# One weight matrix of a decode step, loaded as 7 rows per partition plus three small loads in place of 8 rows per partition

## The chip, the cores and the metric

The kernel runs on one core of one Trainium2 chip. The time is the device time of one execution in microseconds (us). Before the change three runs took 400.60, 400.62 and 400.72 us, with a median of 400.62 us. A separate execution was recorded by the hardware profiler and took 400.47 us. All durations and points in time below come from that one execution and are counted from the start of its span.

## The reference

One token `x` of 1024 numbers goes through a layer norm, then through two branches whose results are added to it. All arrays are bf16.

```python
xn = layernorm(x)
return x + A(xn) + B(xn)

# A: attention over a cache, 32 query heads, 4 key/value heads, 65536 keys of 128 numbers
q = xn @ wq                                   # wq [1024, 4096]
p = softmax(q @ k_cache.T * 128 ** -0.5)      # k_cache, v_cache [4, 65536, 128]
A = (p @ v_cache) @ wo                        # wo [4096, 1024]

# B: a small mixer and a two-layer net
h  = gelu(layernorm(xn) @ w1)                 # w1 [1024, 1024]
g0..g3 = the four quarters of h, each shifted along the sequence by 1, -1, 2, -2, zeros moved in
hs = concatenate(g0..g3) @ w2                 # w2 [1024, 1024]
x1 = xn + hs
B  = x1 + gelu(layernorm(x1) @ w3) @ w4       # w3 [1024, 3584], w4 [3584, 1024]
```

The sequence has length 1, so every shift moves the only token out and a zero in. The left operand of the product with `w2` is therefore a vector of zeros for all inputs. The kernel still loads `w1` and `w2` and does both products, with `g_col`, a column of zeros, as the left operand of the second.

## The kernel before

The kernel reads 169.87 MB once and computes on it while it streams in. On-chip memory holds three buffers, `slot0` to `slot2`, each of 128 partitions by 32768 bf16 values (64 KB per partition, 8 MB in all). A fixed list, `stream`, says what goes through them: `wq`, `w3`, `w12` (`w1` and `w2` side by side in one slot), then for each of 8 units u a block of keys `K u` and a block of values `V u`, each filling a slot, then `wo` and `w4` (in five pieces of 8, 12, 5, 2 and 1 rows per partition). Item i of the list goes to slot i modulo 3.

The kernel writes its work down as one list of operations, `Program`, and then `plan` works out the waits. Each operation has regions that it reads and regions that it writes. The function `region` turns an access into a tensor name, an interval of partitions and an interval of bytes in a partition, and `meet` says whether two regions overlap. An operation waits for every earlier operation of another queue whose region it must not overtake: a write waits for an earlier write to an overlapping region and for earlier readers of it. Each load counts as a queue of its own, so two loads into overlapping regions are ordered by a wait of the second for the landing of the first. The waiting is done by the engine that issues.

All large loads are issued by SyncE (the queue SP), strictly in the order of the list. `load` issues the loads of one item, and `freed(it)` issues the load of the item three places further on, which goes to the same slot, and which therefore waits for the last matmul that reads the item `it`. At the start SP issues `wq`, `w3`, `w1` and `w2` with nothing to wait for. Then comes `K0`, which goes into the slot of `wq` and waits for `compute_wq`; then `V0`, which waits for `compute_w3`; then `K1`, which waits for `compute_w12`; and so on to the end. The tiny load of `x` is issued by ScalarE.

TensorE also works in the order of the list: `compute_wq` (64 matmuls), `compute_w3` (64), `compute_w12` (16 with `w1`, then 16 with `w2`), then unit by unit `scores`, `maxima`, `weights` and `values`. `row_acc` is the helper that adds a product of one column with a 512-wide piece of a weight matrix to the accumulator `psB`. `w2` uses it with all 128 partitions, and so do `wo` and the larger part of `w4` at the end. In `compute_w12` a row number m*8+c of `w2` lies on partition m, as the c-th row there, and the loop runs over c. VectorE transposes the keys in place, reduces and transposes; ScalarE does the exponentials. GpSimd (POOL) sets some constants at the start, `g_col` the last of them, and later places the queries.

All instructions that the list records have the line of a helper: L82 for the vector engines, L89 for loads, L93 for the store, L102 for weight loads of TensorE and L106 for its matmuls.

Of the kernel before, what the change touches and what calls it, by code (L numbers as in the profile page):

```python
# [7 lines left out]
BF16 = mybir.dt.bfloat16  # L8
F32 = mybir.dt.float32
# [5 lines left out]
P = 128  # L15
ROW = 32768
# [3 lines left out]
NARROW = 8  # L20
AHEAD = 5

WIDTH = {F32: 4, BF16: 2}


def region(ap):

    dims, size = list(ap.ap), WIDTH[ap.dtype]
    pitch, rows = dims[0]
    at = ap.offset % pitch  # L30
    last = at + sum((n - 1) * s for s, n in dims[1:])
    p0 = ap.offset // pitch
    return ap.tensor.name, p0, p0 + rows, at * size, (last + 1) * size


def meet(a, b):
# [3 lines left out]
class Op:  # L40
    def __init__(self, engine, emit, reads, writes, alone=False, transfer=False):
        self.engine, self.emit, self.alone, self.transfer = engine, emit, alone, transfer
        self.reads = [region(a) for a in reads]
        self.writes = [region(a) for a in writes]
        self.waits = []
        self.awaited = False


class Program:
# [45 lines left out]
    def mm(self, out, lhsT, rhs, start, stop, pos=(0, 0), size=(P, P)):  # L95

        pe, nc = self.engines["pe"], self.nc
        what = (str(lhsT), size)
        if any(s != size for (_, s), _ in self.held.values()):
            self.held.clear()  # L100
        if pos not in self.held or self.held[pos][0] != what:
            self.add(Op("pe", lambda: pe.ldweights(lhsT, tile_position=pos), [lhsT], []))  # L102
            self.held[pos] = (what, region(lhsT))

        def emit():
            return pe.add_instruction(mybir.InstMatmult(  # L106
                name=nc.get_next_instruction_name(), engine=mybir.EngineType.PE, start_tensor_calc=start,
                stop_tensor_calc=stop, tile_size=size, tile_position=pos, ldweights=False, bass_skip_group_check=True,
                ins=[pe.lower_ap(rhs), pe.lower_ap(lhsT)], outs=[pe.lower_ap(out)]))
        return self.add(Op("pe", emit, [rhs, lhsT], [out]))  # L110
# [96 lines left out]
def kernel(  # L207
# [15 lines left out]
    D = A_x.shape[-1]  # L223
# [6 lines left out]
    DC = D // P  # L230
    FC = F // P
    UKEYS = P * ROW // DH
    assert DH == P and HQ // HKV == 8 and HKV == 4 and D == 1024 and F == 3584 and S == 1
    assert SK == 2 * UKEYS and sum(W4_PIECES) == FC
    NB = 2
    NU = HKV * NB
    SCALE = float(DH) ** -0.5
    LEAD = 8 * (SETS - 1)
    COLS = (P, 32)

    prog = Program(nc)
    pe, dve, act, pool = prog, prog.dve, prog.act, prog.pool

    def sb(name, shape, dtype=F32):
        return nc.alloc_sbuf_tensor(name, list(shape), dtype)

    def ps(name, shape):
        return nc.alloc_psum_tensor(name, list(shape), F32)
# [11 lines left out]
    g_col = sb("g_col", [P, 1], BF16)  # L260
# [14 lines left out]
    sc = ps("sc", [P, SUBS, 512])  # L275
    oacc = ps("oacc", [P, 512])
    pm = [ps(f"pm{i}", [P, 512]) for i in range(2)]
    psB = ps("psB", [P, 512])
# [7 lines left out]
    tiles = {it: slots[i % 3] for i, it in enumerate(stream)}  # L286

    def load(it):
        t = tiles[it]
        if it == "wq":  # L290
            prog.load("sp", t[:], A_wq.rearrange("(p c) n -> p (c n)", c=DC))
        elif it == "w3":
            prog.load("sp", t[:, 0:DC * F], B_w3.rearrange("(p c) f -> p (c f)", c=DC))
        elif it == "w12":
            prog.load("sp", t[:, 0:DC * D], B_w1.rearrange("(p c) n -> p (c n)", c=DC))
            prog.load("sp", t[:, DC * D:2 * DC * D], B_w2.rearrange("(m c) n -> m (c n)", c=DC))
        elif it == "wo":
            prog.load("sp", t[:], A_wo.rearrange("(p j) n -> p (j n)", p=P))
        elif it == "w4":
            w4_v = B_w4.rearrange("(m c) n -> m c n", c=FC)  # L300
            c0 = 0
            for n in W4_PIECES:
                prog.load("sp", t[:, c0 * D:(c0 + n) * D], w4_v[:, c0:c0 + n, :].rearrange("p c n -> p (c n)"))
                c0 += n
        else:
            kind, i = it
            g, b = divmod(i, NB)
            cache = A_k_cache if kind == "K" else A_v_cache
            prog.load("sp", t[:], cache[0, g, b * UKEYS:(b + 1) * UKEYS, :].rearrange("(p ct) d -> p (ct d)", p=P))

    def freed(it):

        n = stream.index(it) + 3
        if n < len(stream):
            load(stream[n])

    load("wq")
    opening = len(prog.ops)

    dve.memset(x_row[:], 0.0)  # L320
    prog.load("act", x_row[0:1, :], A_x[0, 0:1, :])
    load("w3")
    load("w12")

    pool.memset(ident_f[:], 0.0)
    pool.affine_select(out=ident_f[:], in_=ident_f[:], compare_op=ALU.not_equal, fill=1.0, base=0,
# [11 lines left out]
    pool.memset(x_halves[:], 0.0)  # L338
    pool.memset(qdiag[:], 0.0)
    pool.memset(g_col[:], 0.0)  # L340

    def row_acc(j, lhsT, rhs, start=False):
        return pe.mm(psB[32 * j:32 * j + 32, :], lhsT.to_broadcast([P, 32]), rhs, start, False, (0, 32 * j), COLS)

    x_t = p_sb[:, 0:DC * 32].rearrange("p (c j) -> p c j", j=32)
    for a in range(4):
# [4 lines left out]
    def layernorm(src, tag):  # L351
        rowsum = sb(f"ln_rowsum_{tag}", [P, 1])
        dve.reduce_sum(out=rowsum[:], in_=src[:], axis=AX.X)
        at = next_pm()
        pe.mm32(at[:, 0:1], ones_f[:], rowsum[:], True, True)
        negmean = sb(f"ln_negmean_{tag}", [P, 1])
        dve.tensor_scalar(out=negmean[:], in0=at[:, 0:1], scalar1=-1.0 / D, scalar2=None, op0=ALU.mult)
        cen = sb(f"ln_cen_{tag}", [P, DC])
        dve.tensor_scalar(out=cen[:], in0=src[:], scalar1=negmean[:, 0:1], scalar2=None, op0=ALU.add)
        sq = sb(f"ln_sq_{tag}", [P, DC])  # L360
        rowsq = sb(f"ln_rowsq_{tag}", [P, 1])
        dve.tensor_tensor_reduce(out=sq[:], in0=cen[:], in1=cen[:], scale=1.0, scalar=0.0,
                                 op0=ALU.mult, op1=ALU.add, accum_out=rowsq[:])
        pe.mm32(at[:, 1:2], ones_f[:], rowsq[:], True, True)
        std = sb(f"ln_std_{tag}", [P, 1])
        act.activation(out=std[:], in_=at[:, 1:2], func=ACTF.Sqrt, bias=eps_t[:, 0:1], scale=1.0 / D)
        rstd = sb(f"ln_rstd_{tag}", [P, 1])
        dve.reciprocal(out=rstd[:], in_=std[:])
        normed = sb(f"ln_out_{tag}", [P, DC])
        dve.tensor_scalar(out=normed[:], in0=cen[:], scalar1=rstd[:, 0:1], scalar2=None, op0=ALU.mult)  # L370
        rep = sb(f"ln_rep_{tag}", [P, DC, 32], BF16)
        dve.tensor_copy(out=rep[:], in_=normed[:].unsqueeze(2).to_broadcast([P, DC, 32]))
        return normed, rep, negmean, rstd

    xn, xn_rep, negmean1, rstd1 = layernorm(xT, "a")
    _, xn2_rep, _, _ = layernorm(xn, "b")
# [51 lines left out]
        dve.tensor_copy(out=hT[:], in_=h_row[:, ::32])  # L428

    def compute_w12():  # L430
        wt = tiles["w12"][:, 0:2 * DC * D].rearrange("p (w c n) -> p w c n", w=2, c=DC)
        for c in range(DC):
            for q in range(2):
                pe.mm(sc[0:32, q, :], xn2_rep[:, c, :], wt[:, 0, c, 512 * q:512 * (q + 1)], c == 0, c == DC - 1,
                      (0, 0), COLS)
        h1 = p_sb[0:32, 0:1024].rearrange("p (q n) -> p q n", q=2)
        act.activation(out=h1, in_=sc[0:32, 0:2, :], func=ACTF.Gelu_apprx_tanh)
        for c in range(DC):
            for j in range(2):
                row_acc(j, g_col[:], wt[:, 1, c, 512 * j:512 * (j + 1)], start=(c == 0))  # L440
        freed("w12")

    W = ROW // SETS

    nball = [sb(f"nball{i}", [P, NB]) for i in range(2)]
    lall = [sb(f"lall{i}", [P, NB]) for i in range(2)]
    mx = sb("mx", [P, 1])
    m8 = sb("m8", [1, 8])
    rep = sb("rep", [1, P])
    negmg = sb("negmg", [P, 1])  # L450
    wb = sb("wb", [P, NB])
    lw = sb("lw", [P, NB])
    rl = sb("rl", [P, 1])
# [70 lines left out]
    compute_wq()  # L524
    compute_w3()
    compute_w12()
    for u in range(NU):
        g, b = divmod(u, NB)
# [15 lines left out]
    for j in range(32):  # L544
        for h in range(2):
            row_acc(h, oT[:, j:j + 1], tiles["wo"][:, D * j + 512 * h:D * j + 512 * (h + 1)])
    wt = tiles["w4"]
    for c in range(FC - NARROW):
        for j in range(2):
            row_acc(j, hT[:, c:c + 1], wt[:, D * c + 512 * j:D * c + 512 * (j + 1)])  # L550
# [66 lines left out]
```

## Time and profile before

| What | us |
|---|---|
| median of three runs | 400.62 |
| the profiled execution | 400.47 |
| its span | 399.2 |
| `wq` issued by SP, seen as landed by TensorE | 0.94, 22.78 |
| `w3`, `w1` and `w2` issued by SP | 2.31 to 3.67 |
| `K0` issued by SP, seen as landed by VectorE | 28.84, 70.17 |
| `V0` and `K1` issued by SP | 52.21 and 57.92 |
| the store issued | 397.99 |

The profiled execution lies 0.15 us under the median of the runs, and 1.27 us of it lie outside the span. The profile names engines PE (TensorE), PEld (its weight loads), DVE (VectorE), ACT (ScalarE), POOL (GpSimd) and SP (SyncE); a "q" behind a name is the engine's sequencer, which issues DMAs. In the digits by slices each of the 40 digits is the busy share of a fortieth of the span (10 us) in tenths. The names of buffers are given without their numbers, so `slot` is any of the three slots, and `in_B_w_dram` stands for `w1`, `w2`, `w3` and `w4`.

### The profile page before, as it was taken

To read this page: it belongs to the slowest core of one execution; us is meant where nothing else is said; L and a number is where in the kernel's file an instruction comes from. 1 tells how busy PE (TensorE), PEld (TensorE's weight loads), DVE (VectorE), ACT (ScalarE), POOL (GpSimd) and SP (SyncE) were. 2 spreads that over 40 slices of the span, in tenths; PEclk is the share of its full clock that TensorE was granted. 3 is DMA by queue.
4 is the path that set the end of the run, shared out by engine and by line. 5 is a ranking of instruction groups with operands and counts; after the bars stand their busy time and mean duration, and the time that the engine had idled before them with its cause. 6 is when DMAs were issued, how large, how long until landed. Compare 5 with 4: busy or idle time off the path is not lost.

```text
span 399.2 us, 2557 instructions
## 1 busy us (share of the span) xinstructions
PE 223.5 (56%) x1360; PEld 45.8 (11%) x890; DVE 210.2 (53%) x156; ACT 27.6 (7%) x35; POOL 6.2 (2%) x29
## 2 busy tenths in 40 slices
PE   0260970592469256923874196529652946393687
PEld 0210010010100020001001000201020102000233
DVE  0521010975096549653963795259439942793411
ACT  1010030002000200020002000200010011002000
POOL 2000000000000000000000000000000000000000
PEclk9995795598869666978796889568867995698669
DMA  8989999999999999999999999999999999999996
GB/s 329 506 374 419 470 420 427 421 453 479 415 420 427 420 429 427 460 460 420 415 427 420 440 427 455 453 420 420 427 429 440 427 460 435 420 420 427 402 439 259
DMA packets 3760, 170.03 MB, mean 426 GB/s; under 512 B 419, under 2 KB 421, under 8 KB 678
## 3 DMA queue, kind: packets, MB, share of 16 engines
q1 hardware_dynamic: 3744, 169.87, 98.7%
q8 instruction: 9, 0.15, 0.1%
q14 instruction: 1, 0.01, 0.0%
q10 hardware_dynamic: 6, 0.00, 0.0%
HBM read 169.87 MB, written 0.00 MB: 426 GB/s over the span
## 4 chain that ended last, share of the span: by engine, by line
DMA 56%; DVE 24%; PE 14%; another core or an unknown queue 2%; ACT 2%; issue 0%; SPq 0%
DMA slot<-in_A_k_cache_dram 42%; DVE slot L82 19%; PE sc L106 9%; DMA slot<-in_B_w_dram 9%; DMA slot<-in_A_wq_dram 5%; PE oacc L106 4%; DVE p_sb L82 2%; DVE mx L82 2%; ACT p_sb L82 2%; PE pm L122 1%; DVE m L82 0%; DVE rep L82 0%; DVE nball L82 0%; DVE x_halves L82 0%
## 5 line engine op out<-in xcount | busy, mean ns | idle before, releaser
L82 DVE STREAM_TRANSPOSE slot<-slot 128x4096 f32<-128x4096 f32 x32 | 139.4, 4411 | 52.2 <-DMA slot<-in_A_k_cache_dram 52.2
L106 PE MATMUL sc<-slot,qdiag 128*128 128x512 bf16 x512 | 128.2, 410 | 69.0 <-DVE slot L82 68.9
L106 PE MATMUL oacc<-slot,p_sb 128*32 128x512 bf16 x512 | 46.3, 542 | 37.5 <-DVE p_sb L82 18.7
L82 DVE STREAM_TRANSPOSE p_sb<-p_sb 128x2048 bf16<-128x2048 bf16 (+2 forms) x10 | 20.8, 2084 | 38.4 <-ACT p_sb L82 38.3
L82 DVE TENSOR_REDUCE mx<-sc 128x1 f32<-128x2048 f32 x8 | 18.3, 2291 | 29.7 <-PE sc L106 29.7
L102 PEld LDWEIGHTS <-qdiag 128*128 128x128 bf16 x128 | 13.0, 102 | 180.0 <-issue 180.0
L82 ACT ACTIVATE p_sb<-sc,nball 128x2048 bf16<-128x2048 f32 x8 | 15.7, 1967 | 249.9 <-DVE nball L82 249.9
L102 PEld LDWEIGHTS <-p_sb 128*32 128x32 bf16 x512 | 17.3, 131 | 63.3 <-issue 21.8
L106 PE MATMUL sc<-slot,ln_rep_b 128*32 128x512 bf16 (+1 forms) x80 | 16.2, 832 | 8.8 <-DMA slot<-in_B_w_dram 8.6
L82 DVE SCALAR_TENSOR_TENSOR og<-oacc,wb,og 128x512 f32<-128x512 f32 x4 | 3.0, 750 | 19.9 <-PE oacc L106 19.9
L122 PE MATMUL pm<-ident_f,mx 128*1 128x128 f32 x8 | 2.3, 283 | 19.1 <-DVE mx L82 19.1
L106 PE MATMUL psB<-slot,oT 128*32 128x512 bf16 x64 | 9.3, 463 | 1.3 <-DVE oT L82 1.3
L116 PE MATMUL pm<-ol,selx 128*128 128x129 f32 x8 | 2.6, 414 | 10.6 <-DVE ol L82 10.6
L106 PE MATMUL sc<-slot,ln_rep_a 128*32 128x512 bf16 x64 | 6.0, 559 | 4.2 <-DMA slot<-in_A_wq_dram 4.2
L116 PE MATMUL pm<-ln_rowsum_a,msk 128*128 128x1 f32 x2 | 0.6, 363 | 13.5 <-DVE ln_rowsum_a L82 13.5
L82 DVE TENSOR_TENSOR og<-psB,slot 64x512 f32<-64x512 f32 x1 | 0.7, 683 | 13.2 <-PE psB L106 13.2
L82 POOL COPY qdiag<-qx 32x32 bf16<-32x32 bf16 x16 | 3.2, 202 | 277.2 <-PE sc L106 250.5
L82 DVE STREAM_TRANSPOSE p_sb<-x_row 32x256 bf16<-32x256 bf16 x4 | 2.5, 616 | 7.6 <-DMA x_row<-in_A_x_dram 7.6
L122 PE MATMUL pm<-ident_f,rep 1*128 1x1 f32 x8 | 1.9, 235 | 5.0 <-DVE rep L82 5.0
L82 ACT COPY og<-oacc 128x512 f32<-128x512 f32 x4 | 2.3, 585 | 32.9 <-PE oacc L106 32.9
L82 DVE CAST p_sb<-sc 128x512 bf16<-128x512 f32 x1 | 0.7, 691 | 7.4 <-PE sc L106 7.4
L106 PE MATMUL psB<-slot,hT 128*32 128x512 bf16 x40 | 4.5, 379 | 0.0
(86 smaller groups left out, 63.1 us busy)
## 6 DMA issues: line engine op xcount, KB each, us to landing
slot<-in_B_w_dram SPq DMA_DIRECT2D x1, 7168.0 KB, 37.4
slot<-in_B_w_dram SPq DMA_DIRECT2D x3, 2048.0 KB, 43.4
slot<-in_B_w_dram SPq DMA_DIRECT2D x1, 3072.0 KB, 34.5
slot<-in_B_w_dram SPq DMA_DIRECT2D x1, 1280.0 KB, 33.5
slot<-in_B_w_dram SPq DMA_DIRECT2D x1, 512.0 KB, 34.4
slot<-in_B_w_dram SPq DMA_DIRECT2D x1, 256.0 KB, 34.5
slot<-in_A_k_cache_dram SPq DMA_DIRECT2D x8, 42.1
slot<-in_A_v_cache_dram SPq DMA_DIRECT2D x8, 36.9
```

The source lines that it names most:

```text
L82: return program.add(Op(engine, lambda: method(*args, **kw), reads, writes, alone=kw.get("accum_out") is not None))
L102: self.add(Op("pe", lambda: pe.ldweights(lhsT, tile_position=pos), [lhsT], []))
L106: return pe.add_instruction(mybir.InstMatmult(name=nc.get_next_instruction_name(), engine=mybir.EngineType.PE, start_tensor_calc=start, st ...
L116: return self.add(Op("pe", lambda: pe.matmul(out, lhsT=lhsT, rhs=rhs, start=start, stop=stop, tile_position=pos, skip_group_check=True), [ ...
L122: return self.add(Op("pe", lambda: pe.transpose(out, in_, identity), [in_, identity], [out]))
```

## The change

`w1` stays as it is. Of `w2`, rows 0 to 895 are laid out with 7 rows on each of the 128 partitions. The other 128 rows go to the columns behind, in three loads: 16 partitions (0, 4, 8 to 60) with 3 rows each, 5 partitions (2, 6 to 18) with 7 rows each, and 3 partitions (1, 5, 9) with 15 rows each. The columns behind are set to zero first, over partitions 0 to 63 and 15 rows, by one memset on GpSimd; the three loads write over a part of that. The item's loads are written down after the constants of GpSimd now. The product with `w2` takes 7 steps over all partitions and 15 steps over the first 64 partitions, in place of 8 steps, each step being two matmuls. `region` now understands accesses that step over partitions, and gives them the interval from the first to the last partition touched.

```diff
+W2_ROWS = 7
+W2_EXTRA = ((0, 4, 16, 3), (2, 4, 5, 7), (1, 4, 3, 15))
+
 def region(ap):
     dims, size = list(ap.ap), WIDTH[ap.dtype]
-    pitch, rows = dims[0]
+    stride, rows = dims[0]
+    pitch = stride
+    if ap.tensor.name.startswith("slot"):
+        pitch = ROW * WIDTH[BF16] // size
     at = ap.offset % pitch
     last = at + sum((n - 1) * s for s, n in dims[1:])
     p0 = ap.offset // pitch
-    return ap.tensor.name, p0, p0 + rows, at * size, (last + 1) * size
+    return ap.tensor.name, p0, p0 + (rows - 1) * (stride // pitch) + 1, at * size, (last + 1) * size
...
+    W2_REST = (DC + W2_ROWS) * D
...
         elif it == "w12":
             prog.load("sp", t[:, 0:DC * D], B_w1.rearrange("(p c) n -> p (c n)", c=DC))
-            prog.load("sp", t[:, DC * D:2 * DC * D], B_w2.rearrange("(m c) n -> m (c n)", c=DC))
+            prog.load("sp", t[:, DC * D:W2_REST], B_w2[0:P * W2_ROWS, :].rearrange("(m c) n -> m (c n)", c=W2_ROWS))
+            k0 = P * W2_ROWS
+            for p0, step, k, c in W2_EXTRA:
+                prog.load("sp", t[p0:p0 + step * k:step, W2_REST:W2_REST + c * D],
+                          B_w2[k0:k0 + k * c, :].rearrange("(m c) n -> m (c n)", c=c))
+                k0 += k * c
+            assert k0 == D
...
     load("w3")
-    load("w12")
...
     pool.memset(g_col[:], 0.0)
-
-    def row_acc(j, lhsT, rhs, start=False):
-        return pe.mm(psB[32 * j:32 * j + 32, :], lhsT.to_broadcast([P, 32]), rhs, start, False, (0, 32 * j), COLS)
+    more = max(c for _, _, _, c in W2_EXTRA)
+    pool.memset(tiles["w12"][0:64, W2_REST:W2_REST + more * D].bitcast(F32), 0.0)
+    load("w12")
+
+    def row_acc(j, lhsT, rhs, start=False, k=P):
+        return pe.mm(psB[32 * j:32 * j + 32, :], lhsT.to_broadcast([k, 32]), rhs, start, False, (0, 32 * j), (k, 32))
...
     def compute_w12():
-        wt = tiles["w12"][:, 0:2 * DC * D].rearrange("p (w c n) -> p w c n", w=2, c=DC)
+        wt = tiles["w12"]
         for c in range(DC):
             for q in range(2):
-                pe.mm(sc[0:32, q, :], xn2_rep[:, c, :], wt[:, 0, c, 512 * q:512 * (q + 1)], c == 0, c == DC - 1,
+                pe.mm(sc[0:32, q, :], xn2_rep[:, c, :], wt[:, D * c + 512 * q:D * c + 512 * (q + 1)], c == 0, c == DC - 1,
                       (0, 0), COLS)
...
-        for c in range(DC):
+        for c in range(W2_ROWS):
             for j in range(2):
-                row_acc(j, g_col[:], wt[:, 1, c, 512 * j:512 * (j + 1)], start=(c == 0))
+                row_acc(j, g_col[:], wt[:, D * (DC + c) + 512 * j:D * (DC + c) + 512 * (j + 1)], start=(c == 0))
+        for c in range(more):
+            for j in range(2):
+                row_acc(j, g_col[0:64, :], wt[0:64, W2_REST + D * c + 512 * j:W2_REST + D * c + 512 * (j + 1)], k=64)
         freed("w12")
```

## The prediction

> **What bounds the kernel now.** I read the page's busy shares first, then the digits by slices and the DMA queues, then the start of the chain of waits, then the order in which SP issues, and last the single DMA packets in the trace.
>
> ```profile
> PE 223.5 (56%) x1360; PEld 45.8 (11%) x890; DVE 210.2 (53%) x156; ACT 27.6 (7%) x35; POOL 6.2 (2%) x29
> ...
> DMA  8989999999999999999999999999999999999996
> ...
> q1 hardware_dynamic: 3744, 169.87, 98.7%
> q8 instruction: 9, 0.15, 0.1%
> q14 instruction: 1, 0.01, 0.0%
> q10 hardware_dynamic: 6, 0.00, 0.0%
> ```
>
> No compute engine is busy for more than 56% of the span, while SP's queue (q1) keeps the 16 DMA engines busy for 98.7% of it. The kernel is a stream of loads; an idle microsecond of all DMA engines is a microsecond of the result unless a later stage has slack. The next view is the chain of waits up to 75 us, then SP's queue in order of time:
>
> ```profile
> 0.94 21.80 DMA slot<-in_A_wq_dram
> 22.74 0.04 issue
> 22.78 6.04 PE sc L106 x50
> 28.82 0.02 issue
> 28.84 41.31 DMA slot<-in_A_k_cache_dram
> 70.15 0.02 issue
> 70.17 8.77 DVE slot L82 x2
> ```
> ```profile
> 2.31 1.36 SPq L89 DMA_DIRECT2D slot<-in_B_w_dram  x3
> 28.84 0.33 SPq L89 DMA_DIRECT2D slot<-in_A_k_cache_dram  x1
> 52.21 0.33 SPq L89 DMA_DIRECT2D slot<-in_A_v_cache_dram  x1
> 57.92 0.33 SPq L89 DMA_DIRECT2D slot<-in_A_k_cache_dram  x1
> 91.31 0.33 SPq L89 DMA_DIRECT2D slot<-in_A_v_cache_dram  x1
> ```
>
> The reader is to see that K0 is issued at 28.84 and lands 41.31 us later, although its own 8 MB need about 19.4 us (8 packets of 64 KB per engine at 2.42 us). For the other 20 us it stands in the queue behind w3, w1 and w2. That early issue keeps the engines from ever running dry there. The trace's packet records, chained to 16 engines (a packet belongs to the engine whose last packet ends where it begins), give, from the earliest to the latest engine:
>
> ```text
> load      first packet     last data
> w1        38.95 - 39.32    43.81 - 44.18
> w2        43.82 - 45.01    48.68 - 50.36
> K0        48.68 - 50.36    68.00 - 69.72
> last w4   394.15 - 396.05  394.81 - 396.69
> ```
>
> Each load begins where the one before ends, on every engine. The only pauses are the instruction fetches of q8 (16 KB, about 1.05 us each); each sets one engine back by about 1.5 us (a gap of 1.0, and 0.5 on the packet after it). Eight of them fall on eight different engines; the first, at 44.0, makes the slow end of w2. The undelayed engines end at 394.81, the fetching ones at about 396.4 to 396.7, and the kernel ends with the latest.
>
> **The change part by part.**
>
> *Fewer bytes of w2 on every engine.* An engine carried 8 packets of 16 KB (611 ns each). It now carries 8 of 14 KB (about 537 ns, between the 389 ns of the 10 KB packets and the 611) and one of 6 KB (about 236 ns, from 161 ns for 4 KB and 389 for 10). 8 x 611 - 8 x 537 - 236 = 0.35 us less before the next load. That is the whole possible gain, 0.09% of the time, and only if engines without a fetch take the rest. What tells no change from a gain in this kernel is about 0.2%, or 0.8 us.
>
> *The three small loads wait for each other.* They touch different partitions, but `region` gives each one an interval: partitions 0 to 60, 2 to 18 and 1 to 9, all beginning at the same column. The intervals overlap, each load is a queue of its own, so `plan` makes the load of 5 partitions wait for the landing of the load of 16, and the load of 3 for that of 5. SP issues in order, and queued behind on SP are K0, V0 and all that follows. K0 can no longer be issued at 28.84; it comes after two landings, and the first is behind w2 in the same queue. The DMA engines run dry. Step by step, taking the nearest row for each:
>
> - The load of 16 ends on the slowest engine at 50.36 - 0.35 = 50.01.
> - From last data to the waiter: wq 22.40 to 22.78 and the last w4 piece 396.69 to 397.16, so 0.38 to 0.47; I take 0.42.
> - From SP's issue to the first packet of an idle queue: 1.01 for wq on the earliest engine (0.94 to 1.95), 1.34 on the latest; the store took 0.74 (397.99 to 398.73). I take 1.01, a load from SP being the nearer row.
> - The load of 5: 14 KB per engine, 0.54 us at full rate. A packet after a fetch gap takes 0.5 longer, wq's first ones 0.56 to 0.94 longer. Bounds 0.54 and 1.48; I take 1.04, the fetch gap being as short as this pause.
> - Landing to SP: 0.42 again. The load of 3 is issued; SP takes 0.33 to 0.50 per issue (three in 1.36 at 2.31); 0.40. Then K0 is issued and its first packet comes 1.01 later.
>
> K0's earliest packet: 50.01 + 0.42 + 1.01 + 1.04 + 0.42 + 0.40 + 1.01 = 54.31, against 48.68. K0 begins cold: wq's first packets take 3180 ns in place of 2420, so 0.76 more (bounds 0 and 0.94). Sum: 54.31 - 48.68 + 0.76 = 6.4 us. By the lower ends (0.38, 0.74, 0.54, 0.38, 0.33, 0.74, 0) it is 4.4, by the upper ones (0.47, 1.34, 1.48, 0.47, 0.50, 1.34, 0.94) it is 7.9.
>
> Why no more is lost or regained by the fetch delays: before, the first fetch's delay stayed on its engine. Now the load of 16 must land on all engines, so all wait for that engine (this is in the sum, which starts at 50.01), and they start K0 together. The later fetches set other engines back again, so the end still lies about 1.9 us behind an undelayed engine, as before (396.69 against 394.81).
>
> [...]
>
> *The load of 3.* 30 KB go ahead of K0 on three engines (1.13 us), but its packets start an issue (0.40) earlier, so these engines enter K0 0.73 us behind the others. If they get no later fetch, this hides under the 1.5 us that a fetch costs elsewhere: 0. If one does, it adds 0.73. The engine that carried the one-row load of x shows a gap of 76 ns at 7.8 us and no fetch; I take 0.
>
> *The memset, and the wait of the load of 16 for it.*
>
> ```profile
> L82 POOL MEMSET qdiag<- 128x536 bf16 x1 | 0.5, 544 | 0.1
> L82 POOL MEMSET ident_f<- 128x128 f32 x1 | 0.2, 204 | 1.9 <-POOLq L577 1.9
> L82 POOL MEMSET g_col<- 128x1 bf16 x1 | 0.1, 102 | 0.1
> ```
>
> About 0.8 ns an element ((544 - 102) / 536), so 7680 fp32 elements take 6.2 us, from 5.6 to about 11.9. POOL is next needed at 31.54. The load of 16 stands behind w3, w1 and w2, whose data run to 48.7, so its wait until 11.9 is covered. If the memset held up VectorE's preparation (10.56 to about 16.5), 6 us of cover remain before wq lands at 22.78. Price 0.
>
> *More matmuls with w2.* 16 become 44.
>
> ```profile
> L106 PE MATMUL psB<-slot,g_col 128*32 128x512 bf16 x16 | 2.7, 380 | 0.0
> ```
>
> 2.7 / 16 = 0.17 us each, overlapped; 28 more are 4.8 us, and without overlap (380 ns) 10.6. K1 waits for them: issued at 57.92 before, now at 62.7, at most about 69. Its data cannot move before V0's have, which was 87.33 on the earliest engine and is later now. Price 0, with 18 us of cover at the least; TensorE has nothing else until K0 lands. V0, free since 52.21, is issued right behind K0.
>
> Nothing downstream gives the 6.4 us back: every later load is queued well before its predecessor ends (V1 at 91.31, its first packet at 106.68), so the stream has no gap to close, and it shifts whole. Against the profiled execution: 400.47 + 6.4 = 406.9; from the median, 0.15 above that execution, 407.0.
>
> **The rivals.**
>
> *The small loads fall on one engine each.* The store's two rows made two overlapping packets, the load of x one; loads of 5 and 3 rows are not in the trace. On one engine, 70 KB take 2.6 us in place of 0.54 (+2.1), and 90 KB hold K0 back there by 3.4 - 0.4 = 3.0, of which 1.5 may hide under fetches. 400.6 + 6.4 + 2.1 + 1.5 = 410.6. For it: no row of such a shape. Against: the store spread its rows.
>
> *An engine with the load of 3 also gets a fetch.* +0.73: 407.7. For it: half of the engines are hit. Against: the engine of x was not. [...]
>
> *Not slower: the waits are met before the queue is dry.* If the load of 16 did not stand behind w2's packets, all three loads and K0 could be issued by 48.3, when w2 ends on the undelayed engines. Then only the 0.35 us count: 400.3, which is no measurable change. For it: q1 shows nothing of the order inside a load. Against: w1, w2 and K0 follow each other strictly on every engine.
>
> *The waits are shorter than the rows say*, issue to packet as for the store: 400.6 + 4.4 = 405.0.
>
> **How the numbers follow.** Forecast (two waits, 406.1 to 407.9 around 407.0) 0.58; short waits 0.18; load of 3 plus a fetch 0.13; one engine each 0.06; not slower 0.05. The predicted time is 407.0. The range of 404.9 to 408.8 takes in the lower bound of the sum (405.0) and the upper end of it with 7.9 (408.5) and leaves out the single engine and the hidden waits. All cases but one are slower by far over 0.2%: slower 0.95, within 0.2% 0.04, faster 0.01.
>
> **What would show it.** Right: SP issues the load of 5 near 50.4, that of 3 near 52.9 and K0 near 53.3; VectorE's first wait for K0 ends near 76.5; the digit of DMA near 50 us falls; the issue of K1 stays ahead of V0's end; from K0 on all times are 6.4 later. Wrong: K0 issued near 28.84 or before 48; a second stretch of idle DMA; K1 late. The size is wrong if a small load takes more than 1.5 us from its first packet to its landing.

## The result, and the profile after

Four runs of the changed kernel took 407.42 to 408.03 us, with a median of 407.80 us; the kernel before took 400.64 us beside them. The ratio is 1.0177 (95% interval 1.0165 to 1.0189): 7.2 us slower. The profiled execution took 407.42 us, with a span of 406.1. The forecast was 407.0, with a range of 404.9 to 408.8.

The page of the changed kernel, the digits by slices and SP's queue:

```profile
DMA  9989779999999999999999999999999999999896
...
q1 hardware_dynamic: 3792, 169.87, 97.2%
```

The bytes are the same 169.87 MB. The busy share of the stream fell from 98.7% to 97.2%, and the digits show where: the fifth and the sixth slice, about 40 to 61 us, are 7 and 7 in place of 9 and 9. The stretches of 5 us there (columns: stretch, length, busy time and instructions of PE, PEld, DVE, ACT and POOL, granted clock of TensorE, DMA share, GB/s):

```profile
40.00:45.00 5.00, 5.00 (x28) 0.41 (x12) 0.00 (x0) 0.00 (x0) 0.00 (x0) 0.70 1.00 424
45.00:50.00 5.00, 5.00 (x32) 0.50 (x16) 0.00 (x0) 0.00 (x0) 0.00 (x0) 1.00 0.67 283
50.00:55.00 5.00, 4.79 (x27) 0.64 (x10) 1.29 (x2) 1.09 (x2) 0.00 (x0) 1.00 0.10 27
55.00:60.00 5.00, 5.00 (x43) 0.48 (x6) 0.00 (x0) 2.29 (x2) 0.00 (x0) 1.00 1.07 426
```

From 50 to 55 us the DMA engines moved 27 GB/s, a sixteenth of the 426 GB/s of the 5 us after that. The chain of waits says what held them (start, length, what), and SP's own waits say the same in total (waiter, what it waited for, us in total, times, longest):

```profile
12.19 38.20 DMA slot<-in_B_w_dram
50.39 0.02 issue
50.41 2.85 DMA slot<-in_B_w_dram
53.26 0.02 issue
53.27 0.69 SPq L95
53.97 0.04 issue
54.01 22.41 DMA slot<-in_A_k_cache_dram
76.42 0.02 issue
76.44 17.44 DVE slot L88 x4
```
```profile
SPq L95 <- DMA slot<-in_B_w_dram: 39.6, 2, 37.6
...
SPq L95 <- POOL slot L88: 8.4, 1, 8.4
```

SP waits for the memset until 12.19, issues the load of 16, and waits for its landing until 50.41; it issues the load of 5, waits for its landing until 53.27, issues the load of 3, and only then K0, at 54.01. Before, K0 was issued at 28.84 and needed 41.31 us, mostly in the queue. Now it is issued 25 us later and needs 22.41, because only the load of 3 is ahead of it: the queue has run dry.

### The profile page after: what moved, and what is told of

Read it like the earlier page. It is cut to its first block, busy times and chain, and to the rows that moved or that the text cites. A ratio compares the mean times of both kernels' runs of the same rounds, so it can differ in the third digit from the quotient of the medians.

```text
span 406.1 us, 2591 instructions
## 1 busy us (share of the span) xinstructions
PE 227.5 (56%) x1388; PEld 45.8 (11%) x892; DVE 210.2 (52%) x156; ACT 27.6 (7%) x35; POOL 12.7 (3%) x30
## 3 DMA queue, kind: packets, MB, share of 16 engines
q1 hardware_dynamic: 3792, 169.87, 97.2%
HBM read 169.87 MB, written 0.00 MB: 418 GB/s over the span
## 4 chain that ended last, share of the span: by engine, by line
DMA 55%; DVE 24%; PE 13%; another core or an unknown queue 2%; POOL 2%; ACT 2%; issue 1%; SPq 0%; POOLq 0%
DMA slot<-in_A_k_cache_dram 37%; DMA slot<-in_B_w_dram 19%; DVE slot L88 18%; PE sc L112 8%; PE oacc L112 4%; DVE p_sb L88 2%; DVE mx L88 2%; ACT p_sb L88 2%; POOL slot L88 2%; PE pm L128 1%; DVE m L88 0%; DVE rep L88 0%; SPq L95 0%; POOL og L88 0%
## 5 line engine op out<-in xcount | busy, mean ns | idle before, releaser
L112 PE MATMUL oacc<-slot,p_sb 128*32 128x512 bf16 x512 | 47.6, 553 | 37.5 <-DVE p_sb L88 18.8
L112 PE MATMUL sc<-slot,ln_rep_a 128*32 128x512 bf16 x64 | 5.1, 490 | 4.6 <-DMA slot<-in_A_wq_dram 4.6
L88 POOL MEMSET slot<- 64x7680 f32 x1 | 6.5, 6492 | 0.1
L112 PE MATMUL psB<-slot,g_col 64*32 64x512 bf16 (+1 forms) x44 | 5.9, 378 | 0.0
```

The lines of the kernel that those rows point to most:

```text
L88: return program.add(Op(engine, lambda: method(*args, **kw), reads, writes, alone=kw.get("accum_out") is not None))
L112: return pe.add_instruction(mybir.InstMatmult(name=nc.get_next_instruction_name(), engine=mybir.EngineType.PE, start_tensor_calc=start, st ...
```

## The experiments

Unless told otherwise, a kernel is the changed one with the edit shown. The kernel before, run beside them, had medians of 400.54 to 400.59 us; times are medians too.

### Exact regions: the three loads without waits for each other

```diff
-    return ap.tensor.name, p0, p0 + (rows - 1) * (stride // pitch) + 1, at * size, (last + 1) * size
+    step = max(stride // pitch, 1)
+    return ap.tensor.name, p0, p0 + (rows - 1) * step + 1, at * size, (last + 1) * size, step
 def meet(a, b):
-    return a[0] == b[0] and a[1] < b[2] and b[1] < a[2] and a[3] < b[4] and b[3] < a[4]
+    return (a[0] == b[0] and a[3] < b[4] and b[3] < a[4]
+            and bool(set(range(a[1], a[2], a[5])) & set(range(b[1], b[2], b[5]))))
...
-                             if not (w[1] <= r[1] and r[2] <= w[2] and w[3] <= r[3] and r[4] <= w[4])]
+                             if not (w[5] == 1 and w[1] <= r[1] and r[2] <= w[2] and w[3] <= r[3] and r[4] <= w[4])]
```

> The changed kernel with one thing undone: regions of a stepped access name the very partitions touched, so the three small loads no longer wait for each other; layout, bytes, memset and matmuls stay. Theory (the two waits on SP are the whole loss): K0 is issued near 28.9 us again, the queue does not run dry, and the time is that of before less at most the 0.35 us of w2 bytes, 400.3 us, at most 400.7. Rival (the small loads cost something by themselves: small packets, 34 KB more on three engines): above 401.5, up to 401.9 if an engine with 34 KB more (1.25 us at 27.1 KB per us) also gets an instruction fetch. Rival (the loss is in the memset or the matmuls): still near 407.5.

Measured: 400.62 us, ratio 1.0001 (0.9992 to 1.0010). SP's queue in order of time:

```profile
2.34 12.05 SPq L97 DMA_DIRECT2D slot<-in_B_w_dram  x6
28.23 0.35 SPq L97 DMA_DIRECT2D slot<-in_A_k_cache_dram  x1
```

All three small loads are issued by 14.4 us and K0 at 28.23. The whole 7.2 us were the waits; memset, matmuls, layout and the unequal bytes together cost nothing that can be measured. The hoped-for 0.35 us cannot be seen either. In the packet records K0 begins on the earliest engine at 48.20 (48.68 before), but its first packets take 2.65 to 2.70 us in place of 2.42 on eleven of the 16 engines, and the engines that also carry 30 KB come later, so V0's last engine ends at 89.43 (89.06 before).

### The cover: memset and matmuls alone, on the kernel before

`row_acc` takes `k` as in the change.

```diff
+    pool.memset(tiles["w12"][0:64, 2 * DC * D:(2 * DC + 15) * D].bitcast(F32), 0.0)
...
+        for c in range(2 * DC, 2 * DC + 14):
+            for j in range(2):
+                row_acc(j, g_col[0:64, :], tiles["w12"][0:64, D * c + 512 * j:D * c + 512 * (j + 1)], k=64)
```

> The kernel before, its loads untouched, with the memset of 64 x 7680 and 28 more matmuls over 64 partitions added (they read columns that hold zeros, so the product is not changed). Theory (both are covered): 400.6 us, within 0.2; K1's issue moves from 57.92 to about 62. Rival (the memset holds up the preparation, or the matmuls delay the stream): above 401.5, up to 5 more if K1's issue counts.

Measured: 400.56 us, ratio 1.0000 (0.9991 to 1.0009). The memset, and the last group of matmuls with w2:

```profile
5.64 6.49 POOL L82 MEMSET slot<- 64x7680 f32 x1
```
```profile
55.84 5.22 PE L106 MATMUL psB<-slot,g_col 128*32 128x512 bf16 x41
```

The memset took 6.49 us (6.2 forecast), ending at 12.1, and VectorE's first transposes still took 2.52 us for four (2.51 before) with the memset beside them until 12.1. The matmuls end at 61.06, so K1 is issued at 61.09 in place of 57.92, while V0's data run until 87.33 at the least. Both covers hold.

### One wait alone, on the kernel before

`load` takes a list `after` of regions that the load counts as read, so K0 waits for the landing of w2; the loads are those of before.

```diff
+                      after=[tiles["w12"][:, DC * D:2 * DC * D]] if it == ("K", 0) else ())
```

> The kernel before with one wait added and nothing else: K0 is issued only when w2 has landed. It prices a single dry stretch. Theory: w2 lands on the engine with the fetch at 50.36, SP issues at 50.8, K0's first packet at 51.8 against 48.68, and 0.6 more for cold packets: 3.7 us, 404.3 us (404.0 to 404.6). Of the 7.2 us of the change that is the first wait; the other 3.5 belong to the two small loads. Rival (a wait of K0 is cheap and the small loads make the loss): below 402.5.

Measured: 404.58 us, ratio 1.0099 (1.0084 to 1.0113), 4.0 us. SP's queue:

```profile
50.81 0.33 SPq L89 DMA_DIRECT2D slot<-in_A_k_cache_dram  x1
```

K0's first packet came at 51.76, 0.95 us after the issue and 3.1 later than before, and its first packets took 2.4 to 3.8 us. Of the 3.1 us, about 1.7 are not latency at all: all engines now wait for the one that an instruction fetch had set back (w2 ends at 50.32 on that engine, at 48.56 on the first). With the first packets 0.66 us longer on average this accounts for 3.7 us, as expected; the 0.3 beyond it stay open. The edit has a side effect: K1, which goes into the slot of w2, now also waits for the landing of K0 and is issued at 73.08 in place of 57.92. V0's data run until 91.02 at the least, so this holds nothing up.

### One small wait less

```diff
-W2_EXTRA = ((0, 4, 16, 3), (2, 4, 5, 7), (1, 4, 3, 15))
+W2_EXTRA = ((0, 4, 16, 3), (2, 4, 5, 7), (21, 4, 3, 15))
```

> The load of 3 partitions is put on partitions 21, 25 and 29, outside the interval of the load of 5, so it no longer waits for that one; both still wait for the load of 16. Theory (each wait is a dry stretch of its own): the issue of the load of 3 moves from 53.27 to about 51.2, K0's by the same 2.0 us, and the time falls by about 2.0, from 407.8 to 405.8 us. Rival (the queue runs dry once, whatever the number of waits behind): 407.5 to 408.0. Rival (the load of 5 matters only by its data): a fall of about 0.9, 406.9.

Measured: 406.45 us, ratio 1.0146 (1.0132 to 1.0160). SP's waits and its queue:

```profile
SPq L95 <- DMA slot<-in_B_w_dram: 37.6, 1, 37.6
```
```profile
51.98 0.41 SPq L95 DMA_DIRECT2D slot<-in_A_k_cache_dram  x1
```

K0 is issued 2.03 us earlier than in the changed kernel, as expected, but the time fell by 1.35 and not by 2.0. That is more than either rival allows. In its profile one engine ended the load of 3 at 54.37 and began K0 at 56.26, while the other fifteen began it between 53.01 and 55.09. One more run of the same kernel, for this engine:

> A second profile of the kernel with one small wait less, because one engine began K0 at 56.26 us there, 1.9 us after its last packet, while the others began between 53.0 and 55.1, and the time fell by 1.35 us where 2.0 were expected. If the late engine is part of the kernel, it is there again and the time is near 406.4 us; if it was chance, K0 begins on all engines by 55.3 and the time is near 405.8.

Measured, one run: 405.89 us, and K0 began on all engines by 54.96. So the late engine is not fixed in the kernel, and without it the fall is near the 2.0 expected. What held that engine in the first run stays open. This was one run on another chip, while all four of the first took 406.24 to 406.47, so how often it happens, and whether it goes with the chip, is not shown.

### Three loads of 16 rows with the same two waits

```diff
-W2_EXTRA = ((0, 4, 16, 3), (2, 4, 5, 7), (1, 4, 3, 15))
+W2_EXTRA = ((0, 4, 16, 3), (1, 4, 16, 3), (2, 4, 16, 2))
```

> The 128 rows go in three loads of 16 partitions (3, 3 and 2 rows each) with the same two waits. Theory (a load of 5 or 3 partitions takes longer from issue to first packet, 1.57 us against 1.01 to 1.04 for loads on all 16 engines, and occupies SP longer, 0.82 and 0.69 against 0.33 to 0.50): K0's first packet comes near 53.9 in place of 55.05, and no engine has the 30 KB ahead of it; 406.5 us, 406.0 to 406.8. Rival (a restart from a dry queue costs this whatever the shape): only the shorter data count, 0.3 us, 407.4 to 407.6.

Measured: 407.26 us, ratio 1.0167 (1.0153 to 1.0181), 0.5 under the changed kernel. SP's queue of this kernel, then of the changed one (its K0 follows at 54.01):

```profile
50.43 0.49 SPq L95 DMA_DIRECT2D slot<-in_B_w_dram  x1
...
52.67 0.49 SPq L95 DMA_DIRECT2D slot<-in_B_w_dram  x1
...
53.20 0.58 SPq L95 DMA_DIRECT2D slot<-in_A_k_cache_dram  x1
```
```profile
50.41 0.82 SPq L95 DMA_DIRECT2D slot<-in_B_w_dram  x1
...
53.27 0.69 SPq L95 DMA_DIRECT2D slot<-in_B_w_dram  x1
```

Neither side was right. SP needs 0.49 us for each of these loads of 16 rows, 0.82 and 0.69 for 5 and 3. From issue to first packet it is 1.28 us for 16 rows and 1.57 for 5: a part of the time goes with the shape, but a 16-row load on a dry queue is slower than K0 there too (0.95 to 1.23). A wait of this kind, from issue to issue, is 2.24 us here and 2.86 there.

### The same waits on another queue

The three small loads are taken out of `load` and issued by ScalarE after the second layer norm, with the waits as in the changed kernel.

```diff
-                prog.load("sp", t[p0:p0 + step * k:step, W2_REST:W2_REST + c * D],
+            prog.load("act", tiles["w12"][p0:p0 + step * k:step, W2_REST:W2_REST + c * D],
...
     _, xn2_rep, _, _ = layernorm(xn, "b")
+    load_rest()
```

> The changed kernel with its three waits kept, but the three small loads are issued by ScalarE behind the second layer norm, not by SP. Theory (the waits cost only because SP holds back K0 behind them): K0 is issued near 28.9 us, SP's queue does not run dry, 400.4 to 400.8 us. Rival (three loads that land one after the other cost the stream their latency on whatever queue): near 404 to 407. ScalarE is held until about 29 us; its next work, the copy after the product with wq, is not urgent before K0 lands near 70.

Measured: 400.63 us, ratio 1.0002 (0.9993 to 1.0010). SP's queue:

```profile
2.31 1.37 SPq L95 DMA_DIRECT2D slot<-in_B_w_dram  x3
28.93 0.33 SPq L95 DMA_DIRECT2D slot<-in_A_k_cache_dram  x1
```

ScalarE's queue:

```profile
18.51 18.48 ACTq L95 DMA_DIRECT2D slot<-in_B_w_dram  x3
```

The waits are all still there: the three loads are issued at 18.51, 27.54 and 36.29, and the last one's packets end at 41.80, between packets of the large ones. Beside a full stream such a wait is even longer, 9.0 and 8.8 us from issue to issue against 2.86 on the dry queue, and ScalarE is held until 37.0, not 29. It is free even so, because nothing that feeds the stream is queued behind it.

### Disjoint intervals by neighbouring partitions

```diff
-W2_EXTRA = ((0, 4, 16, 3), (2, 4, 5, 7), (1, 4, 3, 15))
+W2_EXTRA = ((0, 1, 16, 3), (16, 1, 5, 7), (21, 1, 3, 15))
```

> The three loads go to partitions 0 to 15, 16 to 20 and 21 to 23, intervals that do not meet, so nothing waits for another small load; the region function stays as the change has it. Theory (the overlap of the intervals is the cause, the placement itself is free): 400.4 to 400.8 us, like the exact regions (400.62). Rival (neighbouring partitions make the small loads slow): above 401. It also shows how long SP takes to issue loads of 5 and 3 neighbouring partitions, 0.82 and 0.69 us for the stepped ones.

Measured: 404.67 us, ratio 1.0103 (1.0089 to 1.0116). The theory was half right: no wait is left, and K0 is issued early. The cost came from elsewhere. SP's queue, and a stretch of 10 us (columns as above):

```profile
29.45 0.36 SPq L95 DMA_DIRECT2D slot<-in_A_k_cache_dram  x1
```
```profile
50.00:60.00 10.00, 9.80 (x68) 1.13 (x16) 1.29 (x2) 3.38 (x4) 0.00 (x0) 1.00 0.59 238
```

The queue is full, yet only 238 GB/s move, against 419 in the same stretch of the kernel before. In the packet records the three packets of 30 KB take 3.96 to 4.18 us (1.16 to 1.20 with exact regions), and the first packet of K0 takes 6.4 to 7.2 us on the twelve engines that got to it early, though these had no 30 KB packet to write.

SP's time, on the other hand, falls. The load of 3 rows:

```profile
12.93 0.25 SPq L95 DMA_DIRECT2D slot<-in_B_w_dram  x1
```

It took 0.69 with exact regions, on every fourth partition. The loads of 16 and 5 rows take SP 0.34 and 0.36 us here, against 0.60 and 0.82 there. So what made SP's part of the small loads long is the step over partitions, more than the number of rows.

### Eight rows, and where they lie

Exact regions, and one load of 8 partitions in place of three:

```diff
-W2_EXTRA = ((0, 4, 16, 3), (2, 4, 5, 7), (1, 4, 3, 15))
+W2_EXTRA = ((0, 8, 8, 16),)
```

> With exact regions, the 128 rows go in one load of 8 partitions with 16 rows each, so 8 engines carry 16 KB more than before and 8 carry 16 KB less (0.6 us each way). The undelayed engines end 1.5 to 1.9 us before those with an instruction fetch. If the 8 engines that carry more are free of fetches: 0.6 us faster, near 400.0. If all 8 are hit by a fetch: 0.6 slower, near 401.2. If hit and free engines are mixed: also up to 0.6 slower. Theory that moving bytes between engines is worth nothing measurable here: 400.6 within 0.2.

Measured: 402.34 us, ratio 1.0053 (1.0039 to 1.0068), slower than any case of the expectation (one of the six runs took 404.38). The 32 KB packets took 1.84 to 2.27 us, and K0's first packets 2.5 to 3.7. Two more runs were to tell placement from bytes. The first takes the exact regions and moves only the three rows of 30 KB next to each other; the second takes the eight rows 4 partitions apart:

```diff
-W2_EXTRA = ((0, 4, 16, 3), (2, 4, 5, 7), (1, 4, 3, 15))
+W2_EXTRA = ((0, 4, 16, 3), (2, 4, 5, 7), (61, 1, 3, 15))
```

> With exact regions (no waits between the small loads, 400.62 us so far), the three rows of 30 KB go to the neighbouring partitions 61, 62 and 63 in place of 1, 5 and 9; nothing else moves. In the run with all small loads on neighbouring partitions they took 3.96 to 4.18 us each, K0's first packets 6.6 to 7.2, and the time was 404.67. Theory (rows for neighbouring partitions are written one after the other, although three engines carry them): 30 KB packets of 2.5 us or more, K0's first packets clearly above 2.7, 402 to 405 us. Rival (the 16 rows on partitions 0 to 15 or the 5 on 16 to 20 made that loss): packets near 1.2 us, 400.4 to 400.9. [...]

```diff
-W2_EXTRA = ((0, 8, 8, 16),)
+W2_EXTRA = ((0, 4, 8, 16),)
```

> One load of 8 partitions with 16 rows each, as in the run that took 402.34 us with partitions 0, 8 to 56, but on partitions 0, 4 to 28. [...] Rival (16 KB more on 8 engines costs this wherever they go): near 402.3. [...]

Measured: 403.82 us for the neighbours, ratio 1.0080 (1.0066 to 1.0094), and 400.92 us for the eight rows 4 apart, ratio 1.0008 (0.9999 to 1.0017). The stretch from 50 to 60 us, first of the neighbours, then of the eight rows:

```profile
50.00:60.00 10.00, 9.79 (x66) 1.20 (x16) 1.29 (x2) 3.38 (x4) 0.00 (x0) 1.00 0.76 315
```
```profile
50.00:60.00 10.00, 9.79 (x67) 1.07 (x12) 1.29 (x2) 3.38 (x4) 0.00 (x0) 1.00 0.97 419
```

With the neighbours the 30 KB packets took 3.19 to 3.48 us and K0's first ones 5.6 to 6.1 on most engines; with eight rows 4 apart every 32 KB packet took 1.213 us and every first packet of K0 about 2.42. So in these runs the partitions that are written decide, not the bytes: on partitions 1, 5 and 9 the same three packets had taken 1.16 to 1.20 us, and on every eighth partition the same eight had taken 1.84 to 2.27. The large packets of other engines slow down too. Why one placement is slow and the other is not, the runs do not show.

The bytes by themselves, 16 KB more on eight engines, cost 0.3 us or nothing: with 0.6 to win or to lose, this fits some of these eight engines being hit by a fetch and others not. That is argued, not shown.

## Why the prediction was right

**The mechanism** was the one forecast: overlapping intervals, two landings on SP ahead of K0, a dry queue, and a stream that shifts whole. The exact regions show that it is all of it, and the loads on ScalarE that it is SP's order that makes it expensive. Step by step:

| Step | forecast | measured |
|---|---|---|
| load of 16, last data | 50.01 | 49.97 |
| SP issues the load of 5 | 50.43 | 50.41 |
| issue to first packet, load of 5 | 1.01 | 1.57 |
| load of 5, first packet to last data | 1.04 | 0.98 |
| landing to SP | 0.42 | 0.31 |
| SP's issue of the load of 3, to K0's issue | 0.40 | 0.74 |
| K0's issue to first packet | 1.01 | 1.04 |
| K0's earliest packet | 54.31 | 55.05 |
| K0's first packets longer by (mean of the 13 engines without the load of 3) | 0.76 | 0.52 |
| sum | 6.4 | 6.9 from these steps; 6.95 between the profiled executions, 7.2 between the medians |

The sum was 0.6 to 0.8 short, and the terms that were mis-sized are those of the small load: its issue to first packet (0.56 short) and SP's time for the load of 3 (0.34 short). Both were taken from loads of 128 rows. The upper ends given, 1.34 and 0.50, did not hold them either. That the total came so near is in part luck: the landing, the load of 5 and the cold first packets came out 0.41 lower together.

**The fetch delays.** The forecast said that the wait takes the first delay in and the later ones come again. The packet records, last data of a load on the earliest and the latest engine:

```text
            V0              whole kernel, latest
before      87.32 - 89.06   396.69
changed     94.19 - 95.44   403.63
```

The earliest engine lost 6.87 us, V0's latest 6.38, the end 6.94: at V0 the delay of 1.7 us was gone and the two ends lay only 1.25 apart, mostly by the engines with the load of 3; at the end it was back. That is also why K0 was seen as landed at 76.44, only 6.27 later than before, while the end moved by 6.95.

**Fewer bytes of w2**, 0.35 us: the engines did begin K0 earlier with exact regions (48.20 against 48.68), but nothing of it can be seen at the end (400.62 against 400.59).

**Covers**: the memset took 6.49 us (6.2 forecast); the 44 matmuls moved K1's issue to 61.20 (62.7 forecast), well before V0's data ended at 94. The group of matmuls in the changed kernel:

```profile
L112 PE MATMUL psB<-slot,g_col x44: 376/376/389, 55.3 to 60.8; 64*32 64x512 bf16 x30, 128*32 128x512 bf16 x14
```

**The rivals.** The small loads on one engine each: no; five packets of 14 KB began between 51.98 and 52.23, three of 30 KB between 54.74 and 55.25. An engine with the load of 3 that also gets a fetch: its three engines began K0 at 56.42 to 56.76, up to 1.7 us after the first. No later fetch of the profiled execution hit one of them up to 385 us: followed from the restart, each of their packets begins within 4 ns of the end of the one before, and the seven fetches from 111.30 to 384.89 all join on to packets of other engines. The waits met before the queue is dry: no, K0 was issued at 54.01. Shorter waits: no, they were longer.

## What to carry to other kernels

In this stream, which was full, a wait on the queue that issues it cost the time from dry to full again, not the size of the load waited for: between the medians one wait cost 4.0 us, a small load with a landing of its own behind it about 1.9 more, and the next 1.35 (1.3 and 1.9 by the single run). Look at the planner's idea of an access before anything else, since an interval around a stepped access can order loads that never touch each other; the cure is an exact region or a queue with nothing urgent behind. And when few partitions are loaded, measure where they lie, since here the small load could slow down the large one behind it: with eight rows of 32 KB the kernel took 400.92 us when they lay on every fourth partition and 402.34 on every eighth, and with three rows of 30 KB 400.62 on partitions 1, 5 and 9 and 403.82 on 61 to 63.

## What was not expected of the hardware

- Rows that different engines wrote to neighbouring partitions took 3.2 to 4.2 us for 30 KB, against 1.16 to 1.20 on every fourth, and the packets of most other engines slowed down with them: K0's first 64 KB took up to 7.2 us against 2.42. Three loads of 256 KB together cost 4.1 us in this way without any wait.
- SP's time for one load did not go with the bytes but with the partitions: 0.33 us for 128 rows, 8 MB (0.41 and 0.58 right behind a small load); every fourth partition 0.49 to 0.60 for 16 rows, 96 KB, 0.82 for 5 rows, 70 KB, and 0.69 for 3 rows, 90 KB; the same three loads on neighbouring partitions 0.34, 0.36 and 0.25 (0.39 for the 3 rows on 61 to 63).
- The first packet of a load came 0.95 to 1.23 us after the issue for 8 MB in 128 rows (0.95 on a queue run dry, the rest right behind a small load), and on a dry queue 1.28 for 16 rows and 1.57 for 5 rows, both on every fourth partition.
